# Attention and feed-forward: one interleaved, planned stream in place of two phases

## The chip, the cores and the metric

The kernel runs on one core of a Trainium2 chip. The metric is device time in microseconds (us) of one launch. TensorE (PE, with its weight loads PEld), VectorE (DVE), ScalarE (ACT), GpSimd (POOL) and SyncE (SP, which here only issues DMAs) each run their own instructions in the order in which they stand, and wait for each other by semaphores.

## The reference

q, k, v have 8 batches x 8 heads x 576 rows x 64; the scores are kept in f32. Per head:

```python
scores = 1/sqrt(64) * q @ k.T
thresh = max(scores, axis=-1) - 0.02
scores = where(scores >= thresh, scores, -1e9)
attn   = softmax(scores)                 # over the keys
x[token, head*64:...] = attn @ v         # 4608 tokens x 512
xn  = x / sqrt(mean(x*x) + 1e-6) * rms_g
g   = xn @ w_gate                        # 512 -> 1536
out = (g * sigmoid(g) * (xn @ w_val)) @ w_out     # 1536 -> 512
```

## The kernel before

**Attention.** The loop over `ip` takes 32 pairs of heads. A pair's q and k (f32) are transposed on PE (L96, L104) and copied out by ACT (L114, L115). Then `j` runs over five chunks of query rows (four of 128, one of 64). For a chunk PE makes the scores of both heads against all 576 keys (L134: 512 keys, L136: 64 keys; f32, each head on 64 rows of the array; each f32 matmul shows as two in the trace), ACT the exponential (L141), DVE a copy of the scores with the row maximum (L148), POOL the threshold (L158), DVE mask times exponential and its row sum (L166). One pair later the masked weights are transposed on PE, 128x128 at a time against an f16 identity (L197), copied out by ACT (L208) and multiplied with v into `ot_ps`, which is head dimension x queries (L219, L222). The reciprocal row sums go through a scratch in DRAM (L180) and come back broadcast over the partitions (L185), and L228 writes `xT`, which holds all 4608 tokens.

**Feed-forward.** The attention pools are released; only then do the row norms of all tokens follow (L299 to L306), and then nine blocks of 512 tokens: gate (L329) and value (L331), 12 x 4 matmuls each, sigmoid on ACT (L333), two products on DVE (L335, L338), and the output projection (L343).

**Order.** The tile framework keeps the written order on each engine and adds the waits; buffers in pools set how far one stage may run ahead. Loads of q and k are issued on SP, those of v and of the weights (cast to f16 in flight) on POOL's queue; the weights come first.

Of the kernel before, what the change touches and what calls it, by code (L numbers as in the profile page):

```python
# [13 lines left out]
DEBUG_OUT = None  # L15
# [3 lines left out]
def kernel(  # L19
# [29 lines left out]
    make_identity(nc, id16)
    ones16 = konst.tile([128, 1], FP16, tag="ones16")  # L50
    nc.vector.memset(ones16, 1.0)
    epsk = konst.tile([1, 1], FP32, tag="epsk")
    nc.vector.memset(epsk, 1e-6)
    zrow = konst.tile([128, S], FP16, tag="zrow")
    nc.vector.memset(zrow, 0.0)
    rmsg = konst.tile([128, 4], FP32, tag="rmsg")
    nc.sync.dma_start(out=rmsg, in_=moe_rms_g.rearrange("(c p) -> p c", p=128))

    wpool = ctx.enter_context(tc.tile_pool(name="wpool", bufs=1))
    wg16 = [wpool.tile([128, DFF], FP16, tag=f"wg{dc}", name=f"wg{dc}") for dc in range(4)]  # L60
    wv16 = [wpool.tile([128, DFF], FP16, tag=f"wv{dc}", name=f"wv{dc}") for dc in range(4)]
    wo16 = wpool.tile([128, NFC, DM], FP16, tag="wo16", name="wo16")
    for dc in range(4):
        nc.gpsimd.dma_start(out=wg16[dc], in_=moe_w_gate[128 * dc:128 * (dc + 1)])
        nc.gpsimd.dma_start(out=wv16[dc], in_=moe_w_val[128 * dc:128 * (dc + 1)])
    nc.gpsimd.dma_start(out=wo16, in_=moe_w_out.rearrange("(fc p) d -> p fc d", p=128))

    xt_pool = ctx.enter_context(tc.tile_pool(name="xt", bufs=1))
    xT = [xt_pool.tile([128, B * S], FP32, tag=f"xT{c}", name=f"xT{c}") for c in range(4)]

    p1 = tc.alloc_tile_pool(name="p1", bufs=1)
    p1ps = tc.alloc_tile_pool(name="p1ps", bufs=1, space=bass.MemoryType.PSUM)
    p1dr = tc.alloc_tile_pool(name="p1dr", bufs=1, space=bass.MemoryType.DRAM)

    def big_ps(name):
        return p1ps.tile([128, S], FP32, tag="big", bufs=2, name=name)

    def emit_loads(ip):
        b, c = divmod(ip, 4)
        st = dict(b=b, c=c, ip=ip)  # L80
        st["qsb"] = p1.tile([128, SC, 2, D], FP32, tag="qsb", bufs=2, name="qsb")
        st["ksb"] = p1.tile([128, SC, 2, D], FP32, tag="ksb", bufs=2, name="ksb")
        st["vsb"] = p1.tile([128, SC, 2, D], FP16, tag="vsb", bufs=2, name="vsb")
        for h in range(2):
            for t_dram, t_sb in ((q, st["qsb"]), (k, st["ksb"]), (v, st["vsb"])):
                eng = nc.gpsimd if t_sb is st["vsb"] else nc.sync
                src = t_dram[b, 2 * c + h, 0:512].rearrange("(sc si) d -> si sc d", si=128)
                eng.dma_start(out=t_sb[:, 0:4, h], in_=src)  # L88
                eng.dma_start(out=t_sb[0:64, 4, h], in_=t_dram[b, 2 * c + h, 512:576, :])  # L89
        return st  # L90

    def emit_head_block(st):
        qt_ps = big_ps("qt_ps")
# [15 lines left out]
        st["qt_ps"], st["kt_ps"] = qt_ps, kt_ps

    def emit_qkt_evac(st):
        st["qt"] = p1.tile([128, S], FP32, tag="qt", bufs=2, name="qt")
        st["kt"] = p1.tile([128, S], FP32, tag="kt", bufs=2, name="kt")
        nc.scalar.activation(out=st["qt"], in_=st["qt_ps"], func=AF.Copy, scale=1.0 / 8.0)  # L114
        nc.scalar.copy(out=st["kt"], in_=st["kt_ps"])  # L115
        st["mcol"] = p1.tile([128, 2, 8], FP32, tag="mcol", bufs=2, name="mcol")
        st["zcol"] = p1.tile([128, 2, 16], FP32, tag="zcol", bufs=2, name="zcol")
        st["wsb"] = [p1.tile([128, SC, S], FP16, tag=f"wsb{h}", bufs=2, name="wsb") for h in range(2)]
        st["ssb"] = {}
        st["esb"] = {}  # L120
        st["thr"] = {}
        st["sp"] = {}
        nc.gpsimd.memset(st["zcol"], 1.0)

    def emit_s_matmul(st, j):
        n = CSZ[j]
        lhs, rhs, sp = {}, {}, {}
        for h in range(2):
            sp[h] = big_ps("sp")
            lhs[h] = st["qt"][64 * h:64 * (h + 1), COF[j]:COF[j] + n]  # L130
            rhs[h] = st["kt"][64 * h:64 * (h + 1), :]
            st["sp", h, j] = sp[h]
        for h in range(2):
            nc.tensor.matmul(sp[h][0:n, 0:512], lhs[h], rhs[h][:, 0:512], start=True, stop=True)  # L134
        for h in range(2):
            nc.tensor.matmul(sp[h][0:n, 512:S], lhs[h], rhs[h][:, 512:S], start=True, stop=True)  # L136

    def emit_exp(st, h, j):
        n = CSZ[j]
        e = p1.tile([128, S], FP16, tag="esb", bufs=3, name="esb")  # L140
        nc.scalar.activation(out=e[0:n], in_=st["sp", h, j][0:n], func=AF.Exp)  # L141
        st["esb"][h, j] = e

    def emit_ttr(st, h, j):
        n = CSZ[j]
        sp = st["sp", h, j]
        sc_sb = p1.tile([128, S], FP32, tag="ssb", bufs=3, name="ssb")
# [238 lines left out]
```

## Time and profile before

| | us |
|---|---|
| median of 3 runs (lowest, highest) | 1108.6 (1103.65, 1116.68) |
| span of the profiled execution, first to last instruction | 1101.2 |
| what lies between that span and the median | 7.4 |
| PE busy | 976.1 (89%) |
| DVE busy | 722.0 (66%) |
| ACT busy | 525.0 (48%) |
| POOL busy | 219.0 (20%) |
| mean granted TensorE clock | 0.880 of full speed |

The profiled execution has no time of its own beside its span; the runs are 2.5 to 15.5 us longer than that span. A busy PE is one with a matmul in flight: matmuls are pipelined, and at a granted clock of 0.50 the same work keeps it busy twice as long. A window's granted clock is a mean over it.

### The profile page before, as it was taken

Reading aid. Unit: us, or ns where it says so; the run is one execution under the profiler, and the core shown is the slowest. Engines: PE = TensorE matmul, PEld = TensorE weight load, DVE = VectorE, ACT = ScalarE, POOL = GpSimd, SP = SyncE. Lnnn points to the kernel's source line nnn. Section 1 sums busy time; section 2 is a strip of 40 time slices with the busy share of each in tenths; the row PEclk is TensorE's granted clock in tenths of the full one; section 3 lists DMA queues with packets and bytes.
Section 4 is the critical chain, followed back from the end, with each engine's and each line's share of the span. In section 5 each row is a group of like instructions: output and inputs, shape, how many; then the busy total and the mean of one; then the engine's idle time right before and its main releaser. Section 6 shows DMA issues by size and latency. Waiting matters only on the chain.

```text
span 1101.2 us, 15548 instructions
## 1 busy us (share of the span) xinstructions
PE 976.1 (89%) x5172; PEld 524.3 (48%) x5172; DVE 722.0 (66%) x1640; ACT 525.0 (48%) x896; POOL 219.0 (20%) x497
## 2 busy tenths in 40 slices
PE   0899998898888999899899899988769999999998
PEld 0455555555445555455555555554214444444443
DVE  0566776677667677776676767776595566555544
ACT  0355554556555555555555556555742223333332
POOL 4122223223232222322222322231000000000000
PEclk9998886889888789886787989897559999999999
DMA  9522222332223222323222323210101110111111
GB/s 179 79 40 52 46 38 40 53 60 40 39 42 52 51 47 38 50 44 60 39 39 39 55 41 59 39 20 15 31 20 48 39 39 22 46 49 39 39 39 39
DMA packets 134227, 50.77 MB, mean 46 GB/s; under 512 B 121721, under 2 KB 123257, under 8 KB 134146
## 3 DMA queue, kind: packets, MB, share of 16 engines
q1 hardware_dynamic: 92530, 40.32, 14.2%
q0 software_dynamic: 41616, 9.45, 9.2%
q8 instruction: 41, 0.67, 0.3%
q14 instruction: 40, 0.33, 0.1%
HBM read 49.55 MB, written 9.62 MB: 54 GB/s over the span
## 4 chain that ended last, share of the span: by engine, by line
PE 63%; DVE 11%; issue 9%; ACT 7%; POOL 7%; DMA 2%; SPq 0%; POOLq 0%; ACTq 0%
PE sp L134 17%; PE gps L329 9%; PE vps L331 9%; PE ops L343 8%; PE wt_ps L197 7%; PE ot_ps L219 7%; DVE ssb L148 6%; ACT esb L141 5%; PE sp L136 4%; POOL vsb L88 3%; POOL vsb L89 3%; DVE irow L305 3%; DVE wsb L166 3%; ACT wtsb L208 2%; DMA ksb<-in_k_dram 2%
## 5 line engine op out<-in xcount | busy, mean ns | idle before, releaser
L148 DVE CUSTOM_DVE_ANT_0 ssb<-sp,zrow 128x576 f32<-128x576 f32 (+1 forms) x320 | 229.5, 753 | 161.9 <-ACT esb L141 161.9
L134 PE MATMUL sp<-kt,qt 64*128 64x512 f32 (+1 forms) x640 | 317.7, 797 | 14.3 <-DVE mcol L148 9.0
L166 DVE SCALAR_TENSOR_TENSOR wsb<-ssb,th,esb 128x576 f16<-128x576 f32 (+1 forms) x320 | 259.2, 817 | 48.8 <-POOL th L158 36.6
L141 ACT ACTIVATE esb<-sp 128x576 f16<-128x576 f32 (+1 forms) x320 | 190.8, 646 | 208.3 <-issue 134.6
L197 PE MATMUL wt_ps<-id,wsb 128*128 128x128 f16 (+3 forms) x1600 | 188.8, 244 | 35.0 <-DVE wsb L166 35.0
L208 ACT COPY wtsb<-wt_ps 128x576 f16<-128x576 f16 (+1 forms) x320 | 193.3, 647 | 42.2 <-PE wt_ps L197 41.9
L158 POOL TENSOR_SCALAR th<-mcol 128x1 f32<-128x1 f32 (+1 forms) x320 | 123.0, 384 | 405.9 <-DVE mcol L148 401.3
L197 PEld LDWEIGHTS <-wsb 128*128 128x128 f16 (+3 forms) x1600 | 118.7, 109 | 112.6 <-DVE wsb L166 50.4
L136 PEld LDWEIGHTS sp<-kt,qt 64*128 64x128 f32 (+1 forms) x640 | 122.3, 226 | 78.9 <-issue 71.2
L134 PEld LDWEIGHTS sp<-kt,qt 64*128 64x128 f32 (+1 forms) x640 | 93.1, 213 | 92.2 <-DVE mcol L148 85.2
L335 DVE TENSOR_TENSOR sl<-gps,sg 128x512 f32<-128x512 f32 x108 | 74.6, 691 | 92.0 <-ACT sg L333 92.0
L219 PE MATMUL ot_ps<-wtsb,vsb 128*64 128x512 f16 (+1 forms) x320 | 123.4, 430 | 0.0
L333 ACT ACTIVATE sg<-gps 128x512 f32<-128x512 f32 x108 | 64.5, 597 | 122.7 <-PE gps L329 122.7
L329 PE MATMUL gps<-xn,wg 128*128 128x512 f16 x432 | 113.0, 383 | 9.3 <-DVE xn L319 9.3
L331 PE MATMUL vps<-xn,wv 128*128 128x512 f16 x432 | 112.1, 382 | 0.0
L136 PE MATMUL sp<-kt,qt 64*128 64x64 f32 (+1 forms) x640 | 110.4, 285 | 0.0
L343 PE MATMUL ops<-wo,h 128*128 128x512 f16 x432 | 94.7, 379 | 0.0
L338 DVE TENSOR_TENSOR h<-vps,sl 128x512 f16<-128x512 f32 x108 | 74.6, 691 | 11.0 <-PE gps L329 0.9
L96 PE MATMUL qt_ps<-id,qsb 128*128 128x128 f32 (+1 forms) x160 | 27.7, 287 | 52.8 <-issue 30.3
L329 PEld LDWEIGHTS <-wg 128*128 128x128 f16 x432 | 42.6, 99 | 61.9 <-issue 11.9
L114 ACT ACTIVATE qt<-qt_ps 128x576 f32<-128x576 f32 x32 | 20.8, 651 | 104.6 <-PE qt_ps L96 104.6
L331 PEld LDWEIGHTS <-wv 128*128 128x128 f16 x432 | 42.5, 98 | 52.5 <-issue 2.3
(38 smaller groups left out, 585.3 us busy)
## 6 DMA issues: line engine op xcount, KB each, us to landing
rzbc<-zscr SPq DMA_DIRECT2D x64, 144.0 KB
out_dram<-osb SPq DMA_DIRECT2D x36, 256.0 KB
qsb<-in_q_dram SPq DMA_DIRECT2D x64, 128.0 KB
ksb<-in_k_dram SPq DMA_DIRECT2D x64, 128.0 KB
vsb<-in_v_dram POOLq DMA_DIRECT2D x64, 64.0 KB, 2.8
zscr<-rzt SPq DMA_DIRECT2D x256, 0.6 KB
irb<-irdr SPq DMA_DIRECT2D x9, 256.0 KB
wg<-in_moe_w_gate_dram POOLq DMA_DIRECT2D x4, 384.0 KB, 10.0
```

Source lines behind the costliest of these rows:

```text
L134: nc.tensor.matmul(sp[h][0:n, 0:512], lhs[h], rhs[h][:, 0:512], start=True, stop=True)
L136: nc.tensor.matmul(sp[h][0:n, 512:S], lhs[h], rhs[h][:, 512:S], start=True, stop=True)
L141: nc.scalar.activation(out=e[0:n], in_=st["sp", h, j][0:n], func=AF.Exp)
L148: nc.vector.tensor_tensor_reduce(out=sc_sb[0:n], in0=sp[0:n], in1=zrow[0:n], scale=1.0, scalar=-3.0e38, op0=ALU.add, op1=ALU.max, accum_ou ...
L158: nc.gpsimd.tensor_scalar(out=th[0:n], in0=st["mcol"][0:n, h, j:j + 1], scalar1=-tau, scalar2=None, op0=ALU.add,)
L166: nc.vector.scalar_tensor_tensor(out=st["wsb"][h][0:n, j], in0=st["ssb"][h, j][0:n], scalar=st["thr"][h, j][0:n], in1=st["esb"][h, j][0:n] ...
L197: nc.tensor.transpose(wt_ps[0:nk, COF[qc]:COF[qc] + nq], st["wsb"][h][0:nq, qc, COF[kc]:COF[kc] + nk], id16[0:nq, 0:nq],)
L208: nc.scalar.copy(out=wt[0:nk], in_=st["wt_ps", h, kc][0:nk])
L219: nc.tensor.matmul(ot[64 * h:64 * h + 64, 0:512], lhs, rhs[0:nk, 0:512], start=first, stop=last)
L329: nc.tensor.matmul(g_ps, wg16[dc][:, fsl], xn[dc], start=(dc == 0), stop=(dc == 3))
L331: nc.tensor.matmul(v_ps, wv16[dc][:, fsl], xn[dc], start=(dc == 0), stop=(dc == 3))
L343: nc.tensor.matmul(o_ps, hsb[fc][:, otc[tb]:otc[tb] + 128], wo16[:, fc], start=(fc == 0), stop=(fc == NFC - 1),)
```

## The change

The whole kernel is written anew. What is computed stays, in another order and with other parts:

- The unit is a **step**: 128 query rows x one pair of heads. The 576 rows of a batch give four chunks of 128 ("m"); the left 64 rows of two batches form one more chunk ("v"). That is 36 chunks x 4 pairs = 144 steps, chunk by chunk, so that a chunk's 512 features of x are complete after four steps.
- q is scaled by -1/8, so the row minimum plus tau is the negated threshold. DVE's reduction (L414) reads PSUM and leaves the negated scores in `ssb`. POOL adds tau (L421).
- For head 0 of a step ACT masks with Prelu of slope 1e30 (L430) and takes the exponential (L434). For head 1 ACT takes the exponential (L443), and POOL makes the mask (L457) and multiplies (L462). In the first 16 steps both heads go the first way.
- The masked weights of a step (128 x 1152, f16) are transposed by one DMA on SP (L473) into `wt`, nine blocks of 128. PE multiplies them as the stationary operand with v (L488; L493 for a "v" chunk), whose 64 columns have 64 columns of ones beside them: the row sums come out as columns of `ot`. DVE divides (L514, L515).
- The row norm is taken per chunk: ACT squares and sums (L526), POOL raises to -1/2 (L531), DVE scales (L534), one DMA transposes 128x512 (L537).
- The feed-forward of a group of chunks (512, 256 or 128 tokens) is cut into pieces (gate L576, value L581, output L615), and the pieces stand between the attention's steps; sigmoid is written with tanh (L588), and DVE's products are L591 and L596. Three PSUM banks (`ring`) serve gate, value, output and the transposes of q and k (L266, L292, L309); scores have four banks, `ot` one.
- Weights are loaded in f32 by SP (L671) and multiplied by rms_g into f16 on POOL (L674) between the first steps.
- A planner (`order_ops`) orders all operations before the program is written: each has an engine, a cost out of a table, a priority and its dependencies; of the operations that could start first the one of lowest priority number is taken.

```diff
-    for ip in range(NPAIR + 2):          # attention, pair by pair
-        ... emit_wt_transposes, emit_s_matmul, emit_wt_evac, emit_exp, emit_ttr, emit_th, emit_stt
-    p1ps.release(); p1.release(); p1dr.release()
-    for t in range(NTC): ...             # row norms, then feed-forward
+    def emit_s(s):                       # "m" chunk
+        for lo, n, src in ((512, MAIN, kT[b % 2][p]), (448, TAIL, kTt[b % 2][:, p])):
+            for h in range(2):
+                hs = slice(64 * h, 64 * h + 64)
+                nc.tensor.matmul(s_ps[h][:, lo:lo + n], qT[b % 2][p][hs, 128 * c:128 * (c + 1)],
+                                 src[hs], start=True, stop=True)
+    ...
+    nc.vector.tensor_tensor_reduce(
+        out=ssb[a][:, h], in0=s_ps[h][:, 448:1024], in1=zrow, scale=1.0, scalar=3.0e38,
+        op0=ALU.add, op1=ALU.min, accum_out=mx[m][:, h:h + 1])
+    ...
+    nc.sync.dma_start_transpose(out=wt[s % NWT], in_=wsb[s % NW].rearrange("p h s -> p (h s)"))
+    ...
+    for j in range(5):
+        nc.tensor.matmul(ot[:, cs], w[:, 4 * h + j], v_rhs(b % 2, p, 5 * h + j),
+                         start=(j == 0), stop=(j == 4))
+    ...
+    for s, (ci, p) in enumerate(steps):
+        so = s_of[s] = emit_s(s)
+        emit_softmax(s, so)
+        emit_av(s)
+        if p % 2:
+            emit_half(s)
+        if p == NP - 1:
+            xt_op[ci] = emit_x(ci, s, gi % NXT, 128 * j)
+            if ci in last_of:
+                emit_ffn(last_of[ci] % NXT, [...], s + 5, PACE)
+    ...
+    seq = order_ops(ops, {"R": 3})
+    with tc.manual_schedule():
+        for o in seq:
+            o.fn(o)
+PACE, FIRST, WAYS = 16.0, 16, ("pg",)
```

Where the order moves, PE first, inside the attention. Before (`sp` scores, `wt_ps` transposed weights, `ot_ps` output):

```order
L219 LDWEIGHTS vsb
L219 MATMUL ot_ps<-wtsb,vsb 64x512
L222 LDWEIGHTS vsb
L222 MATMUL ot_ps<-wtsb,vsb 64x64
L134 MATMUL sp<-kt,qt 128x512 x2
L136 MATMUL sp<-kt,qt 128x64 x2
L197 LDWEIGHTS wsb
L197 MATMUL wt_ps<-id_63,wsb 128x128
```

After, on PE about a third of the way through (`s_ps` scores, `wt` weights from the DMA, `ring` transposed k and value piece):

```order
L380 MATMUL s_ps_177<-kTt_99,qT_1_87 128x64
L488 LDWEIGHTS wt_128
L488 MATMUL ot<-va_103,wt_128 128x128
...
L266 MATMUL ring_181<-id_61,kn_77 128x128 x4
L581 LDWEIGHTS wv_69
L581 MATMUL ring_179<-xnT_147,wv_69 128x512
...
L380 MATMUL s_ps_176<-kT_2_96,qT_2_88 128x512
```

No transpose of weights is left on PE, and feed-forward stands between two steps' scores. The `wt` that is read belongs to a step four to five before the scores next to it. The first gate piece stands behind the scores of step 18; behind those of the last step stand 192 feed-forward matmuls of 128 columns, 164 of 256, 72 of 512 and three steps' products with v.

DVE before, inside a pair:

```order
L148 ISA ssb,mcol<-sp,zrow 128x576
L148 ISA mcol 128x1
L148 ISA ssb,mcol<-sp,zrow 128x576
L148 ISA mcol 128x1
L166 SCALAR_TENSOR_TENSOR wsb,zcol<-ssb,th,esb 128x576 x2
L228 TENSOR_TENSOR xT_101<-ot_ps,rzbc 128x576
```

DVE after:

```order
L414 ISA ssb_104,mx_107<-s_ps_176,zrow 128x576
L414 ISA mx_107 128x1
L414 ISA ssb_104,mx_107<-s_ps_177,zrow 128x576
L414 ISA mx_107 128x1
L514 RECIPROCAL rz_131<-ot 128x4
L515 TENSOR_TENSOR xsb_133<-ot,rz_131 128x256
L591 SCALAR_TENSOR_TENSOR sl_154<-th_151,ring_181 128x512
L596 TENSOR_TENSOR hf_160<-ring_179,sl_154 128x512
```

The mask has left DVE, and the feed-forward's products stand between the reductions of two steps.

SP after, in the same stretch (`kn`, `qn`: loads for a later batch):

```order
L262 DMA kn_77<-in_k_dram 128x4x64 x2
L262 DMA qn_75<-in_q_dram 128x4x64 x2
L473 DMA_TRANSPOSE wt_128<-wsb_123 128x9x128
L473 DMA_TRANSPOSE wt_129<-wsb_124 128x9x128
L473 DMA_TRANSPOSE wt_125<-wsb_122 128x9x128
L537 DMA_TRANSPOSE xnT_147<-xn_145 128x4x128
```

Loads, transposes and stores share SP's queue in one order: 144 transposes of nine blocks and 36 of four stand among some 210 plain DMAs.

## Rows read from the trace of the kernel before

**Rows 1.** The page: the span, and PE's busy time, share and instructions.
```profile
span 1101.2 us, 15548 instructions
PE 976.1 (89%) x5172; PEld 524.3 (48%) x5172; DVE 722.0 (66%) x1640; ACT 525.0 (48%) x896; POOL 219.0 (20%) x497
```

**Rows 2.** Stretches: length; PE, PEld, DVE, ACT, POOL busy (count); clock; DMA share; GB/s.
```profile
842.00:873.00 31.00, 31.00 (x145) 14.04 (x144) 19.06 (x28) 9.51 (x16) 0.00 (x0) 1.00 0.12 43
...
200.00:300.00 100.00, 88.53 (x540) 51.32 (x538) 72.85 (x193) 57.04 (x99) 28.54 (x65) 0.92 0.28 49
20.00:28.00 8.00, 2.77 (x10) 1.79 (x10) 0.00 (x0) 0.74 (x2) 1.11 (x2) 1.00 1.20 194
779.00:811.00 32.00, 19.23 (x36) 2.94 (x36) 26.59 (x10) 27.05 (x47) 0.00 (x0) 0.50 0.06 17
```

**Rows 3.** Order of time on PE: start, duration, what; one pair of heads.
```profile
404.56 2.08 PE L134 MATMUL sp<-kt,qt 64*128 64x512 f32 x4
406.43 0.53 PE L136 MATMUL sp<-kt,qt 64*128 64x64 f32 x4
...
408.55 1.37 PE L134 MATMUL sp<-kt,qt 64*128 64x512 f32 x3
409.51 0.33 PE L136 MATMUL sp<-kt,qt 64*128 64x64 f32 x2
...
410.45 0.99 PE L197 MATMUL wt_ps<-id,wsb 128*128 128x128 f16 x10
...
420.25 0.83 PE L96 MATMUL qt_ps<-id,qsb 128*128 128x128 f32 x5 [1.01 <-issue]
421.01 0.86 PE L104 MATMUL kt_ps<-id,ksb 128*128 128x128 f32 x5
```

**Rows 4.** Two short stretches of PE: length, busy (count), granted clock, DMA share, GB/s.
```profile
404.50:406.90 2.40, 2.40 (x11) 0.50 0.57 128
...
408.50:410.50 2.00, 1.95 (x9) 1.00 0.01 2
```

**Rows 5.** Order of time on PE: the first scores.
```profile
28.60 2.08 PE L134 MATMUL sp<-kt,qt 64*128 64x512 f32 x4 [0.73 <-ACT kt L115]
```

**Rows 6.** The chain that ended last: the last block's output projection.
```profile
1087.12 10.38 PE ops L343 x48
```

**Rows 7.** Order of time on DVE and POOL: reductions, mask, threshold.
```profile
403.07 0.76 DVE L148 CUSTOM_DVE_ANT_0 ssb<-sp,zrow 128x576 f32<-128x576 f32 x1 [2.14 <-ACT esb L141]
...
403.75 0.75 DVE L148 CUSTOM_DVE_ANT_0 ssb<-sp,zrow 128x576 f32<-128x576 f32 x1
...
404.00 0.21 POOL L158 TENSOR_SCALAR th<-mcol 128x1 f32<-128x1 f32 x1 [3.12 <-DVE mcol L148]
...
404.43 0.82 DVE L166 SCALAR_TENSOR_TENSOR wsb<-ssb,th,esb 128x576 f16<-128x576 f32 x1
...
404.67 0.64 POOL L158 TENSOR_SCALAR th<-mcol 128x1 f32<-128x1 f32 x1 [0.46 <-DVE mcol L148]
```

**Rows 8.** Groups by shape: line, engine, count; busy us, mean ns; idle before.
```profile
L141 ACT ACTIVATE esb<-sp 128x576 f16<-128x576 f32 x256 | 152.9, 648 | 171.2 <-issue 100.0 <-PE sp L136 67.5 <-DVE wsb L166 1.7
...
L335 DVE TENSOR_TENSOR sl<-gps,sg 128x512 f32<-128x512 f32 x108 | 74.6, 691 | 92.0 <-ACT sg L333 92.0
...
L333 ACT ACTIVATE sg<-gps 128x512 f32<-128x512 f32 x108 | 64.5, 597 | 122.7 <-PE gps L329 122.7
...
masks.py:199 POOL TENSOR_SCALAR_AFFINE_SELECT id<-id 128x128 f32<-128x128 f32 x1 | 0.3, 290 | 0.0
```

**Rows 9.** DMA queues: packets, MB, share; issues: count, KB, us to landing.
```profile
q1 hardware_dynamic: 92530, 40.32, 14.2%
q0 software_dynamic: 41616, 9.45, 9.2%
...
vsb<-in_v_dram POOLq DMA_DIRECT2D x64, 64.0 KB, 2.8
```

**Rows 10.** Order of time on PE: the first transpose.
```profile
22.56 1.38 PE L96 MATMUL qt_ps<-id,qsb 128*128 128x128 f32 x5 [22.56 <-DMA qsb<-in_q_dram]
```

More of the change, by code (lines that the diff above doesn't have):

```diff
@@ L51 @@
[L51 to L69, printed above, removed]
@@ L111, in emit_qkt_evac @@
[L111 to L123, printed above, removed]
@@ new lines, with gated, add @@
+    ops = []
+    gates = []
+    s_of = {}
+    def gated(o, step):
+        gates.append((o, step))
+        return o
+    def add(eng, cost, prio, deps, fn, **kw):
+        o = Op(eng, cost, prio, deps, fn, **kw)
+        ops.append(o)
+        return o
+    chunks = []
+    for i in range(B // 2):
+        chunks += [("m", 2 * i, c) for c in range(4)]
+        chunks.append(("v", i, 0))
+        chunks += [("m", 2 * i + 1, c) for c in range(4)]
+    steps = [(ci, p) for ci in range(len(chunks)) for p in range(NP)]
@@ new lines, with setup, consts, vconst @@
+    first_step = {}
+    for s, (ci, p) in enumerate(steps):
+        kind, b, _ = chunks[ci]
+        if kind == "m":
+            first_step.setdefault(b, s)
+    last_s = {}
+    last_sv = {}
+    last_av = {}
+    n_load = {"q": 0, "k": 0}
+    tr_of = {"q": [], "k": []}
+    k_ready = {}
+    kt_ready = {}
+    q_ready = {}
+    qv_ready = {}
+    v_ready = {}
+    tail_load = {}
+    def setup():
+        o_id = add("POOL", 2000.0, -100, [], lambda o: make_identity(nc, id32))
+        def consts(o):
+            nc.vector.memset(zrow, 0.0)
+            nc.vector.memset(mhalf, -0.5)
+        def vconst(o):
+            for i in range(2):
+                nc.vector.memset(va[i][:, :, 10:13], 1.0)
+                for j in (4, 11):
+                    nc.vector.memset(va[i][64:128, :, j], 0.0)
+                for j in (5, 12):
+                    nc.vector.memset(va[i][0:64, :, j], 0.0)
+        o_c = add("DVE", 300.0, -100, [], consts)
+        o_v = add("DVE", 2000.0, -90, [], vconst)
+        o_g = add("SP", 70.0, -50, [], lambda o: nc.sync.dma_start(
+            out=rmsg, in_=moe_rms_g.rearrange("(c p) -> p c", p=128)), dma=100.0)
+        return o_id, o_c, o_v, o_g
@@ L354 @@
+    for o, step in gates:
+        if step > 0:
+            o.deps.append(s_of[int(step)])
+    for h in range(2):
+        ttr_of[len(steps) - 1, h].opens = (3 + 2 * h, 4 + 2 * h)
+    seq = order_ops(ops, {"R": 3})
+    global LAST_SEQ
+    LAST_SEQ = seq
+    with tc.manual_schedule():
+        for o in seq:
+            o.fn(o)
+PACE = 16.0
+FIRST = 16
+WAYS = ("pg",)
+PRELU = AF.Prelu
+PRELU_KW = dict(alpha=1.0e30)
 _INS = ['q', 'k', 'v', 'tau', 'moe_w_gate', 'moe_w_val', 'moe_w_out', 'moe_rms_g']
```

743 lines of the change are left out of this document (491 added, 252 removed).

## The prediction, made before the changed kernel was run

> **What bounds the kernel now.** I read the page's first part first: PE is busy 976 us of a span of 1101.2, every other engine far less [rows 1]. Then the busy time by stretches [rows 2]. In the feed-forward (842 to 873) PE is busy without a break at full granted clock; in the attention (200 to 300) it is busy 88.5 us of 100 at clock 0.92; between the two, 779 to 811, it works 19 us of 32 at half clock while the row norms of all tokens are made. So PE is the bound in both big phases, but in the attention part of its time is half clock, and part is work that is no product of the reference: the transposes of the weights. That half clock doubles a duration is seen in two neighbouring pieces of one pair: the scores that begin at 404.56 take 1.87 us until their tail of 64 keys starts, at clock 0.50; those at 408.55 take 0.96, at 1.00 [rows 3, 4]. The scores at 28.60 last as the half-clock ones do [rows 5].
>
> The sum is made against the profiled execution. It has its span, 1101.2; the median of the runs, 1108.6, lies 7.4 above, and I add those 7.4 to every span below.
>
> **PE's work after the change, at full clock.** Counts are those of the new order.
> - Scores of a step: half of the half-clock piece, which is 406.43 + 0.53 - 404.56 = 2.40 us for both heads [rows 3], so 1.20. 128 steps of an "m" chunk are 154 us; a "v" chunk's step does the same twice (16 x 2.40 = 38). Sum 192.
> - Products with v: 1600 matmuls of 128 columns, each with a load of its own. No row has this form. From below: a 512-column matmul of the output projection takes 10.38 / 48 = 0.216 us [rows 6], a quarter is 0.054. From above: ten weight transposes of the same size, loads included, take 0.99 [rows 3], 0.099 each. The first price supposes that the loads hide, the second holds what they cost there; I take the middle, 0.077: 123 us.
> - Transposes of q and k: 304, at (421.01 - 420.25) / 5 = 0.152 [rows 3]: 46 us.
> - Feed-forward: (576 + 432) matmuls of 512 columns at 0.216, 480 of 256 at 0.108, 192 of 128 at 0.077: 218 + 52 + 15 = 285 us.
>
> Sum 645 us, against 976 busy now. What goes is the weight transposes, the half clock, and scores of half-empty chunks (five per batch and pair, now four and a half).
>
> **The other engines stay below that.** DVE: 288 reductions at 403.75 - 403.07 = 0.68 [rows 7] are 196 us; the feed-forward's products at 0.691 for 512 columns [rows 8], 144 of them, are 100, and the 168 of 256 or fewer at some 0.43 (estimate, between a half and the whole) 72; what remains (division, norm: 72 and 36 small operations) is below 80. Sum some 450. ACT: 427 passes over 576 columns at 0.648 [rows 8] are 277, the tanh at 0.597 or less some 80, copies and squares 144 x 0.65 = 94: some 450. POOL now gets the mask and the multiply of one head per step, of which before shows nothing of this size. From below, an operation on one column takes 0.21 [rows 7]; from above, a select over 128 columns takes 0.29 [rows 8], times 4.5 for 576 is 1.3, and twice that for the one with two inputs, 2.6. With a threshold of 0.21 to 0.64 a step costs POOL between 0.6 and 4.5 us, PE's mean step in the middle is 4.7 (below). So POOL is not the bound even at its upper end, but close to it there. The threshold is 0.21 beside a reduction that reads PSUM, and 0.64 beside the mask on DVE [rows 7], which the change removes; I count the lower one.
>
> **The DMA transposes** have no row at all. A step moves 128 x 1152 x 2 = 294,912 bytes. From below: at the 194 GB/s that loads reach [rows 2], 1.5 us. From the packets: the hardware queue spends 0.142 x 16 x 1101.2 / 92530 = 0.027 us an engine and packet, the software queue 0.039 [rows 9]. In pieces of 256 bytes (a row of 128) a transpose is 72 packets an engine, 1.9 to 2.8 us; in pieces of 64 bytes, 288, 7.8 us. I take 2, since the order shows one instruction for nine blocks with rows of 128. With the 36 smaller ones there are 160 equivalents: 320 us, and the other transfers fill at most what all do now, 0.234 x 1101 = 258 [rows 9]. That is 578 of some 730: no bound. As latency they cost nothing: a step's products with v stand four to five steps behind its scores, some 20 us; the reductions (1.4), threshold (0.2), ACT (3 x 0.65), POOL and a transfer with its landing (2.8 for a load [rows 9]) need about 11. If that cover is gone, PE stands at the first load of `wt`, with all feed-forward behind it.
>
> The Trainium skill speaks against this part. In "VectorE: DVE Perf Modes", section "The three transpose paths", a 128x128 transpose takes 1309 ns by the DMA crossbar and 390 on TensorE, and its table of rules prefers TensorE where PSUM will do as the target; nine blocks in a row would be 11.8 us, and the DMA work alone 160 x 11.8 = 1,890 us, not 320. No row here shows such a transfer.
>
> **The sum, in three stretches.**
> - Until the feed-forward starts (19 steps). PE now waits until 22.56 for its first q, behind the weights [rows 10]; afterwards q and k are in front, and I put the first scores at 13 (a landing of 2.8 for loads, three transposes with their copies, and slack). A step then is a loop: scores, two reductions, next scores. At half clock, which [rows 5] shows for a start, that is 2.40 + 1.36 + 0.3 for hand-offs = 4.1; at full clock 2.9. I take 3.9: 13 + 19 x 3.9 = 87. PE does 48 us of its 645 in it.
> - The middle. What stands behind the last scores is 192 x 0.077 + 164 x 0.108 + 72 x 0.216 + 30 x 0.077 = 50, so the middle holds 645 - 48 - 50 = 547, or 4.4 us a step for 125 steps. While DVE reduces (1.4) PE has 3.2 us of other work a step, so the loop through DVE closes in time. Hand-offs that don't: now PE idles 11.5% of the attention [rows 2]; most engines then waited on one pair, here steps overlap, and I take 5%, with clock 0.98: 547 / 0.95 / 0.98 = 588.
> - The end: 50 and a last copy and store, 55.
>
> 87 + 588 + 55 = 730, plus 7.4: **737 us**, 0.66 of before.
>
> **Rivals.**
> 1. *Everything cheaper.* Products with v at 0.054, no idle in the middle, clock 1.00, early steps at 2.9. Total work 604; 68 + 514 + 50 + 7 = 639. For it: PE in the feed-forward shows no break at all [rows 2]. Against: the mix has many short waits.
> 2. *PE in the middle as in today's attention.* Busy 0.885, clock 0.92, early steps at 4.1: 547 / 0.814 = 672; 91 + 672 + 57 + 7 = 827. For it: hand-offs among four engines, three shared PSUM banks, strict order. Against: the breaks now lie between pairs (PE idle 1.01 before the transposes of q at 420.25 [rows 3]), and there are no such boundaries afterwards.
> 3. *The feed-forward doesn't overlap.* The order puts it between steps, but if each piece only comes through where attention stands still, the change doesn't do what it says: 13 + 144 x 3.9 + 285 + 7 = 867.
> 4. *The DMA transposes bound it* (the side of slower). One mechanism: the crossbar path moves small pieces, the sixteen DMA engines fill, `wt` comes late, PE waits at each load of it. Time is 160 x (time of one) + 258 + some 20; it is slower than before from 5.2 us for one, and at 7.8 gives 1,526. For it: no row excludes small packets; those of the two queues now average 436 and 227 bytes [rows 9]. Against: 256-byte rows are as natural, and give 2 us. At the skill's 11.8 us it would be some 2,170; of the 9% below I give that price 3.
>
> **Chances and range.** Forecast (670 to 790) 60%, rival 1 14%, rival 2 12%, rival 3 5%, rival 4 9%. The range of 8 in 10 goes from rival 1 to rival 3: 640 to 865, which leaves out rival 4 and the rims. A change of 1% (11 us) is about what a measurement of this kernel can tell from none. Faster by over 1%: 90%; within 1%: 1%; slower by over 1%: 9%.
>
> **What would show it.** PE busy near 645 us and the bound (over 85% of a span near 730); matmuls of `ot` at 0.05 to 0.1 apart; scores of a step in 1.2 us at clock 1.00; the first gate matmul near 87 us; some 55 us from the last scores to the end; DMA busy share near 0.8 at most, transposes landing within 5 us. It is wrong if PE waits most for `wt` (rival 4), if the time of PE before L380 ends on DVE for more than a tenth of the middle (rival 2), or if POOL turns out busiest, its two operations having cost over 4 us a step.

## The result, and the profile of the changed kernel

Measured on one chip, four runs each: **701.8 us** (700.12 to 703.25) for the changed kernel, 1106.4 (1103.65 to 1116.68) for the kernel before. The ratio is 0.633, 95% interval 0.630 to 0.637. The forecast was 737, range 640 to 865. The profiled execution of the changed kernel has a run time of 701.5 us and a span of 699.8, so what lies around the span is 1.7 us here, where 7.4 were added. (The 7.4 set one execution's span against the median of others; in all later runs, of both kernels, 1.7 to 2.2 us lie around an execution's own span.) The ratios here and below are taken over executions in the faster of two states in which the chip ran these kernels; in the session of experiments 5 to 8 three of the seven executions of the kernel before were in the slower one, and the 693.0 of experiment 10 was.

First the page of the changed kernel: the span, then busy time, share and instructions of each engine; the granted clock and the DMA share in 40 slices; the two DMA queues; the chain of waits by engine.

```profile
span 699.8 us, 13808 instructions
PE 641.8 (92%) x4864; PEld 388.6 (56%) x4864; DVE 428.8 (61%) x1080; ACT 455.2 (65%) x789; POOL 529.3 (76%) x570
...
PEclk9897889998899999999999999999999999999999
DMA  9899997487686546975897455977596454444410
...
q1 hardware_dynamic: 275344, 81.83, 59.1%
q0 software_dynamic: 14912, 6.30, 8.7%
...
PE 45%; POOL 29%; issue 8%; DMA 6%; ACT 6%; DVE 4%; SPq 1%; POOLq 0%; DVEq 0%; ACTq 0%
```

PE is busy 642 us where it was 976 [rows 1] and still has the largest share. New is POOL: 529 us where it had 219, and 29% of the chain. The chain names PE and POOL together, which says that two engines are close to their limit; it does not say what either is worth. Experiments 2 and 3 settle that.

Next the stretches, in the columns of [rows 2]: before the first scores (their first matmul begins at 11.1), until the first gate matmul (90.7), the middle until the last scores' matmul is done (646), the end.

```profile
0.00:11.10 11.10, 2.44 (x10) 1.70 (x11) 2.93 (x12) 2.48 (x3) 6.03 (x14) 1.00 0.94 144
11.10:90.70 79.60, 62.06 (x374) 40.31 (x373) 31.27 (x87) 53.72 (x90) 49.67 (x58) 0.82 1.05 206
90.70:646.00 555.30, 529.03 (x4027) 310.98 (x4025) 363.04 (x881) 377.26 (x639) 466.52 (x492) 0.98 0.67 123
646.00:699.80 53.80, 48.26 (x458) 35.61 (x457) 31.55 (x102) 21.79 (x58) 7.11 (x8) 1.00 0.21 52
```

In the middle PE works 529 of 555 us at clock 0.98, where the attention of before stood at 88.5% and 0.92 [rows 2]; POOL works 467, 84%.

Then the order of time on PE (start, duration, what), in three places: the first gate; one step's scores; ten products with v among feed-forward pieces near the end.

```profile
90.71 1.03 PE L576 MATMUL ring<-xnT,wg 128*128 128x256 f16 x4
...
299.99 1.13 PE L380 MATMUL s_ps<-kT,qT 64*128 64x512 f32 x4
300.95 0.33 PE L380 MATMUL s_ps<-kTt,qT 64*128 64x64 f32 x4
301.22 1.04 PE L581 MATMUL ring<-xnT,wv 128*128 128x512 f16 x4
...
650.67 0.73 PE L488 MATMUL ot<-va,wt 128*128 128x128 f16 x10
651.24 0.60 PE L576 MATMUL ring<-xnT,wg 128*128 128x256 f16 x4
```

Matmuls are pipelined, so a price is the distance from one start to the next, not a duration. A step's scores take 301.22 - 299.99 = 1.23 us. Ten products with v take 651.24 - 650.67 = 0.57, so 0.057 each, their loads included.

POOL's order of time in the same place, where the steps' operations follow each other almost without a gap:

```profile
299.11 1.28 POOL L462 TENSOR_TENSOR wsb<-wsb,esb 128x576 f16<-128x576 f16 x1
300.46 0.22 POOL L421 TENSOR_SCALAR nth<-mx 128x2 f32<-128x2 f32 x1
300.78 1.73 POOL L457 TENSOR_SCALAR wsb<-ssb,nth 128x576 f16<-128x576 f32 x1
302.59 1.27 POOL L462 TENSOR_TENSOR wsb<-wsb,esb 128x576 f16<-128x576 f16 x1
303.85 1.71 POOL L457 TENSOR_SCALAR wsb<-ssb,nth 128x576 f16<-128x576 f32 x1
```

The mask takes 1.73 us, the multiply 1.28, the threshold 0.22: 3.2 us a step, against 4.4 that a step of the middle lasts (555.3 / 125). Last the page's row of the DMA transposes: count, and us from issue to landing.

```profile
wt<-wsb SPq DMA_TRANSPOSE x144, 3.3
```

### The profile page after: what moved, and what is told of

Its sections match the earlier page's. It is cut to its first block, busy times and chain, and to the rows that moved or that the text cites. A ratio compares the mean times of both kernels' runs of the same rounds, so it can differ in the third digit from the quotient of the medians.

```text
span 699.8 us, 13808 instructions
## 1 busy us (share of the span) xinstructions
PE 641.8 (92%) x4864; PEld 388.6 (56%) x4864; DVE 428.8 (61%) x1080; ACT 455.2 (65%) x789; POOL 529.3 (76%) x570
## 3 DMA queue, kind: packets, MB, share of 16 engines
q1 hardware_dynamic: 275344, 81.83, 59.1%
## 4 chain that ended last, share of the span: by engine, by line
PE 45%; POOL 29%; issue 8%; DMA 6%; ACT 6%; DVE 4%; SPq 1%; POOLq 0%; DVEq 0%; ACTq 0%
POOL wsb L457 13%; PE s_ps L380 12%; POOL wsb L462 8%; PE ring L615 8%; PE ring L576 6%; PE ring L581 6%; DMA wt<-wsb 5%; PE ot L488 5%; POOL nth L421 2%; ACT ssb L430 2%; DVE ssb L414 2%; PE ring L266 2%; PE ot L493 2%; POOL wv L674 2%; ACT wsb L434 1%
## 5 line engine op out<-in xcount | busy, mean ns | idle before, releaser
L414 DVE CUSTOM_DVE_ANT_0 ssb<-s_ps,zrow 128x576 f32<-128x576 f32 x288 | 208.4, 753 | 135.8 <-PE s_ps L380 91.9
L457 POOL TENSOR_SCALAR wsb<-ssb,nth 128x576 f16<-128x576 f32 x128 | 221.6, 1731 | 9.1
L380 PE MATMUL s_ps<-kT,qT 64*128 64x512 f32 x512 | 172.3, 676 | 15.0 <-DVE mx L414 9.9
L462 POOL TENSOR_TENSOR wsb<-wsb,esb 128x576 f16<-128x576 f16 x128 | 163.4, 1277 | 11.3 <-ACT esb L443 1.9
L443 ACT ACTIVATE esb<-ssb,nth 128x576 f16<-128x576 f32 x128 | 98.8, 772 | 95.0 <-POOL nth L421 94.6
L430 ACT ACTIVATE ssb<-ssb,nth 128x576 f32<-128x576 f32 x160 | 121.0, 762 | 12.4 <-POOL nth L421 12.4
L581 PE MATMUL ring<-xnT,wv 128*128 128x512 f16 (+2 forms) x528 | 108.4, 328 | 2.6 <-DVE sl L591 1.8
L488 PE MATMUL ot<-va,wt 128*128 128x128 f16 x1280 | 97.4, 226 | 14.6 <-DMA wt<-wsb 12.0
L434 ACT ACTIVATE wsb<-ssb 128x576 f16<-128x576 f32 x160 | 107.6, 680 | 3.9
L576 PE MATMUL ring<-xnT,wg 128*128 128x512 f16 (+2 forms) x520 | 107.3, 329 | 0.9 <-ACT qT L273 0.7
L588 ACT ACTIVATE th<-ring 128x512 f32<-128x512 f32 (+2 forms) x130 | 63.0, 488 | 57.2 <-PE ring L576 57.0
L488 PEld LDWEIGHTS <-wt 128*128 128x128 f16 x1280 | 80.3, 101 | 34.8 <-DMA wt<-wsb 21.8
L591 DVE SCALAR_TENSOR_TENSOR sl<-th,ring 128x512 f32<-128x512 f32 (+2 forms) x130 | 71.9, 553 | 45.1 <-ACT th L588 43.1
L421 POOL TENSOR_SCALAR nth<-mx 128x2 f32<-128x2 f32 x144 | 34.6, 240 | 81.6 <-DVE mx L414 61.6
L380 PEld LDWEIGHTS s_ps<-kTt,qT 64*128 64x128 f32 x512 | 62.3, 196 | 60.3 <-issue 58.5
L615 PE MATMUL ring<-wo,hf 128*128 128x512 f16 x396 | 90.3, 379 | 0.0
L596 DVE TENSOR_TENSOR hf<-ring,sl 128x512 f16<-128x512 f32 (+2 forms) x132 | 73.7, 558 | 12.1 <-PE ring L581 2.4
L380 PEld LDWEIGHTS s_ps<-kT,qT 64*128 64x128 f32 x512 | 48.8, 194 | 57.3 <-DVE mx L414 26.5
L581 PEld LDWEIGHTS <-wv 128*128 128x128 f16 x624 | 54.6, 98 | 33.4 <-issue 4.6
L576 PEld LDWEIGHTS <-wg 128*128 128x128 f16 x624 | 55.2, 98 | 31.4 <-issue 1.7
L615 PEld LDWEIGHTS <-hf 128*128 128x128 f16 x432 | 40.7, 98 | 44.9 <-issue 0.2
L380 PE MATMUL s_ps<-kTt,qT 64*128 64x64 f32 x512 | 54.0, 252 | 0.0
```

Of the source, the lines that this page charges most:

```text
L380: nc.tensor.matmul(s_ps[h][:, lo:lo + n], qT[b % 2][p][hs, 128 * c:128 * (c + 1)], src[hs], start=True, stop=True)
L414: nc.vector.tensor_tensor_reduce(out=ssb[a][:, h], in0=s_ps[h][:, 448:1024], in1=zrow, scale=1.0, scalar=3.0e38, op0=ALU.add, op1=ALU.min, ...
L430: nc.scalar.activation(out=ssb[a][:, h], in_=ssb[a][:, h], func=PRELU, scale=-1.0, bias=nth[m][:, h:h + 1], **PRELU_KW)
L434: nc.scalar.activation(out=wsb[s % NW][:, h], in_=ssb[a][:, h], func=AF.Exp)
L443: nc.scalar.activation(out=esb[es], in_=ssb[a][:, h], func=AF.Exp, scale=-1.0, bias=nth[m][:, h:h + 1])
L457: nc.gpsimd.tensor_scalar(out=wsb[s % NW][:, h], in0=ssb[a][:, h], scalar1=nth[m][:, h:h + 1], scalar2=None, op0=ALU.is_le)
```

## The experiments

They are numbered as they ran; 8, 10 and 11 stand last. The ratio of each is to the kernel before, run on the same chip. The medians of the kernel before in those sessions, 1101.8 to 1111.3, lie up to 5 us on either side of the 1106.4 above, so a small difference from the change is judged by the ratios. Unless said otherwise, the fence holds rows of that kernel's page, as shown above.

**1. Products with v made twice.** What is PE's work worth?

```diff
-            for h in range(2):
+            for h in (0, 0, 1, 1):
```

> Edit: every product with v is made twice (the second time over the first), same order otherwise. It adds 1600 matmuls of 128 columns with their loads on TensorE, 1600 x 0.057 us (ten take 0.57 us in the trace of the change) = 91 us, and nothing elsewhere. Theory A (TensorE's own work sets the middle; it is busy 95% there): nearly all of it shows, 702 + 75 to 95, so 775 to 797 us. Rival B (GpSimd's mask and multiply set the pace: they are 21% of the chain that ended last and GpSimd is 84% busy in the middle): TensorE has slack behind them, 702 to 730 us.

Measured: 750.1 us (745.8 to 753.0), ratio 0.682 [0.677, 0.688].

```profile
span 746.6 us, 17008 instructions
PE 701.0 (94%) x6464; PEld 459.5 (62%) x6464; DVE 428.2 (57%) x1080; ACT 456.7 (61%) x789; POOL 529.2 (71%) x570
...
PE 68%; POOL 17%; issue 5%; DMA 4%; ACT 2%; DVE 2%; SPq 0%; POOLq 0%; DVEq 0%; ACTq 0%
```

1600 products at 0.057 are 91 us of work; the time rose by 48, which is neither of the two expected bands. PE's busy time rose by only 59. The mean clock went from 0.966 to 0.988, which is worth some 14 us of the missing 32 (an estimate: 642 x 0.966 / 0.988); the other 18 no row here accounts for. Of the 59, 12 went into PE's gaps, whose share of the span fell from 8% to 6%. PE's added work counts for about half.

**2. POOL's mask made twice in every second step.** What is POOL's work worth?

```diff
-                        nc.gpsimd.tensor_scalar(...)        # mask, head 1
+                        for _ in range(1 + s % 2):
+                            nc.gpsimd.tensor_scalar(...)
```

> Edit: GpSimd makes the mask of every second step twice (same result), same order otherwise: 64 x 1.73 = 111 us more on GpSimd, nothing elsewhere. Theory A (TensorE sets the middle): GpSimd goes from 467 of 555 us in the middle to some 577, so it just becomes the longer one; 702 + 20 to 40, so 720 to 745 us. Rival B (GpSimd sets the pace): all 111 us show, 800 to 815 us.

Measured: 803.4 us (801.4 to 804.2), ratio 0.731 [0.725, 0.736]. 64 masks at 1.73 are 111 us on POOL, and 102 of them came through. The page:

```profile
PE 677.4 (84%) x4864; PEld 403.3 (50%) x4864; DVE 431.4 (54%) x1080; ACT 454.8 (57%) x789; POOL 639.4 (80%) x634
...
POOL 51%; PE 24%; issue 10%; DMA 6%; DVE 4%; ACT 4%; SPq 1%; POOLq 0%; DVEq 0%; ACTq 0%
```

And the group of PE's products with v in the stretch 90 to 690 (L489 here, L488 in the change; behind the bars: busy us, mean ns; idle before, and what ended it):

```profile
L489 PE MATMUL ot<-va,wt 128*128 128x128 f16 x1000 | 78.2, 229 | 51.3 <-DMA wt<-wsb 48.8 <-DVE mx L414 1.6 <-DVE xsb L516 0.7
```

The idle is put down to the DMA, but the transposes land as soon as before (3.3 us): they start late, behind POOL. In the change the same group has 13 us of idle, 12 for `wt` (below). SP's longest waits there before a transpose are for POOL: for the threshold they grew from 110 to 148 us, for the multiply from 31 to 66. The expectation that POOL has room fell. More work on POOL costs nearly its whole length, at a lower clock of PE as well (0.927).

**3. No mask on POOL: both heads by Prelu on ACT.**

```diff
-PACE, FIRST, WAYS = 16.0, 16, ("pg",)
+PACE, FIRST, WAYS = 16.0, 16, ("pp",)
```

> Edit: head 1 of a step goes the way of head 0 in all steps (both masks by ScalarE), GpSimd keeps only the small operations; the planner orders anew. GpSimd loses 128 x (1.73 + 1.28) = 385 us of 529, ScalarE gains 128 x (0.76 + 0.68 - 0.77) = 86 us to some 541. Theory A: TensorE's work is the same, 690 to 715 us. Rival B: the pace is freed, 640 to 670 us.

Measured: 685.6 us (684.0 to 689.3), ratio 0.625 [0.620, 0.629], between the two expected bands.

```profile
span 682.3 us, 13340 instructions
PE 636.5 (93%) x4864; PEld 391.2 (57%) x4864; DVE 416.8 (61%) x1080; ACT 532.4 (78%) x917; POOL 143.7 (21%) x314
...
PE 66%; ACT 13%; DMA 8%; DVE 5%; issue 4%; POOL 3%; SPq 1%; DVEq 0%; ACTq 0%; POOLq 0%
```

386 us leave POOL, ACT takes 77 more, and 16 us are gained (some 10 by the ratios): PE, now 66% of the chain, stands right behind. Experiments 2 and 3 together give the size that the chain could not: POOL has no slack for more, and giving its mask to ACT is worth 1 to 2%.

**4. The mask on DVE.** `WAYS = ("pd",)`.

> Edit: the mask and multiply of head 1 in one operation on VectorE instead of two on GpSimd; the planner orders anew. VectorE gains 128 x 0.82 = 105 us to some 534, GpSimd loses 385. Theory A: 690 to 715 us as long as VectorE's longer queue doesn't delay the reductions on which the next scores wait. Rival B: 640 to 670 us. A third outcome, VectorE as the new limit through its place in the loop scores - reduction - scores: 720 to 760 us.

Measured: 698.8 us (697.8 to 700.1), ratio 0.636 [0.632, 0.640]; no difference from the change. POOL fell to 180 us, DVE rose to 505: a POOL without the mask gains nothing that can be told if DVE has to make it.

**5. Every DMA transpose made twice**, the second into a buffer that nobody reads. Does the DMA bound it?

```diff
             nc.sync.dma_start_transpose(out=wt[s % NWT], ...)
+            nc.sync.dma_start_transpose(out=wt2[s % NWT], ...)
```

> Edit: every DMA transpose of a step is issued twice, the second into a buffer that nobody reads; same order otherwise. From the packets of the change (its hardware queue: 275344 packets, some 194000 of them transposes, 0.023 us each an engine) one transpose is some 1.7 us of all 16 DMA engines, so 144 x 1.7 = 245 us more on engines that are 68% busy of 700 now: 476 + 245 = 721 us of DMA work, over 1.0 in the first 90 us. My pricing of the prediction (a DMA bound from the sum of transfers): 730 to 790 us. Rival: a transpose is latency, hidden by the four to five steps' lead, 702 to 712 us. Second rival: it costs SyncE 1.3 us to issue one, and the queue, not the engines, becomes late; then the waits for wt on TensorE grow from 34 us while the DMA share stays below 0.9.

Measured: 766.1 us (762.2 to 769.1), ratio 0.696 [0.691, 0.701], within the band priced from the sum of transfers.

```profile
span 762.8 us, 13999 instructions
PE 655.7 (86%) x4864; PEld 395.9 (52%) x4864; DVE 427.9 (56%) x1080; ACT 456.5 (60%) x789; POOL 530.0 (69%) x570
...
DMA  9999999999999998899999999999999998979611
...
q1 hardware_dynamic: 445840, 124.31, 88.3%
q0 software_dynamic: 14912, 6.30, 7.4%
```

q1's time grew from 0.591 x 699.8 = 414 us to 0.883 x 762.8 = 674, so 144 transposes cost 260, **1.8 us each** with all sixteen engines. Now the DMA row is full: 0.957 x 762.8 = 730 us. In the change the same sum is 0.678 x 699.8 = 474. PE's waits for `wt` grew from 16 to 55 us. That fits DMA engines that set the end, but it does not settle it: the share is no hard limit (it was 1.05 in the second stretch of the change), the transposes land in 3.5 us, little later than before (3.3), and SP's queue, on which each takes some 1.3 us to issue, got 144 more as well. The run does not part the engines from the queue.

**6. The feed-forward in lumps.** `PACE = 1.0` in place of 16: a group's pieces come close behind each other.

> Edit: PACE 16 to 1, so the planner no longer spreads a group's feed-forward over 16 steps but lets all of it in as early as it can; work is the same. If the even spread is what makes the gain (TensorE's feed-forward under the attention's waits): lumps of some 31 us of feed-forward, limited by three PSUM banks, and between them steps at the attention's own pace (GpSimd 3.5 us a step), 780 to 880 us. Rival: the planner starts whatever can start first, so attention and feed-forward still mix and it stays at 702 to 740 us.

Measured: 777.4 us (776.1 to 778.4), ratio 0.706 [0.701, 0.711], between the two expected bands and close to the upper one; PE busy 687 us at a mean clock of 0.929. The same instructions in a less even order cost 76 us, of which 45 are PE's longer busy time.

**7. The kernel before, with its weights transposed by DMA.** Is that alone the gain? PE's transposes (L197) and ACT's copies (L208) go; behind each mask stands

```diff
+        nc.sync.dma_start_transpose(
+            out=st["wtT"][h][:, :, COF[j]:COF[j] + n], in_=st["wsb"][h][0:n, j])
```

> Edit on the kernel before, one part of the change alone: the masked weights are transposed by DMA (per head and chunk of query rows, 128 or 64 x 640), in place of TensorE's transposes and ScalarE's copies; everything else stays. It takes 1600 transposes (189 us busy, some 150 at full clock) from TensorE and 320 copies (193 us) from ScalarE. Theory: TensorE bounds the attention of before, 22.7 us a pair, so a pair falls by 3 to 5 us: 1102 - 95 to 160 = 940 to 1005 us. Rival 1: the chain scores - exponential - reduction - mask of one chunk sets the pair (VectorE is busy 16.6 of 22.8), 1060 to 1110 us. Rival 2: the transposes come late and TensorE waits for them at the first product of a pair, slower than 1110 us.

Measured: 1286.5 us (1285.6 to 1287.9), ratio 1.169 [1.162, 1.176]. Slower, which only rival 2 allowed, and its mechanism is not what the trace shows: PE waits 3 us in all for the transposes. PE lost 1600 matmuls but only 38 us of busy time, at a mean clock of 0.717 (before 0.880). What grew are two waits: PE's for DVE's reductions before L141 (L134 before), from 9 to 226 us, and DVE's for POOL's threshold before the mask, from 37 to 150, some 5 us at each of 31 pairs. One such break, from that trace in order of time:

```profile
612.96 0.81 POOL L94 DMA_DIRECT2D vsb<-in_v_dram  x1 [7.28 <-PE ot_ps L218]
...
615.71 0.49 POOL L165 TENSOR_SCALAR th<-mcol 128x1 f32<-128x1 f32 x2
...
615.95 0.84 DVE L173 SCALAR_TENSOR_TENSOR wbuf<-ssb,th,esb 128x576 f16<-128x576 f32 x1 [4.46 <-POOL th L165]
...
618.27 2.75 PE L141 MATMUL sp<-kt,qt 64*128 64x512 f32 x4 [4.38 <-DVE mcol L155]
```

POOL stands at a load of v, which waits for the products that read the old v; the thresholds come behind the four loads, the mask behind the thresholds, the next reductions behind the mask, and PE idles 4.4 us. No run takes these loads off POOL's queue, so what this order costs is not measured.

**9. The same, with the DMAs of the reciprocal row sums on POOL's queue,** in case they stand on SP's queue behind a transpose that waits for its mask.

```diff
-                nc.sync.dma_start(out=scr[h, :, a], ...)
+                nc.gpsimd.dma_start(out=scr[h, :, a], ...)
-            nc.sync.dma_start(out=rzbc[64 * h:64 * (h + 1)], ...)
+            nc.gpsimd.dma_start(out=rzbc[64 * h:64 * (h + 1)], ...)
```

> Edit on the kernel before with DMA transposes (1286.5 us): the reciprocal row sums go out to scratch and come back through GpSimd's queue instead of SyncE's, where the second broadcast stood behind a transpose that waits for the mask of the next pair. If that place in SyncE's queue is what made it slower (VectorE's division waits for the broadcast, the reductions stand behind the division, the next scores behind those; TensorE idles 4.4 us there and falls to half clock): a pair falls from 28.5 us to under 22.7, 950 to 1100 us in all. Rival: the half clock of a TensorE that is left with little work is the cause, it stays at 1200 to 1290 us.

Measured: 1293.9 us (1290.9 to 1295.4), ratio 1.163 [1.158, 1.169], clock 0.715. The place on SP's queue alone is not the cause. The test is not clean, since it put 164 us of issuing on POOL (218 to 382 us busy), where the thresholds stand.

**12. Experiment 7 with PE's transposes back, unread.** Products still take the DMA's copy; ACT copies nothing.

> The kernel before with its weights transposed by DMA (1286.5 us, mean clock 0.717) gets its 1,600 weight transposes on PE back, but nobody reads what they make: the products still take the DMA's copy, and ACT copies nothing. It tells the half clock from the loop. Theory C (with little to do PE stands at half clock, and that makes the pair 28.5 us long): PE gets work between the scores, the mean granted clock rises to 0.80 or more, and the time falls in spite of the added work, to 1110-1230 us. Rival D (a loop through DVE, POOL and the DMA transposes sets the pace; the clock only follows): 1260-1310 us, whatever the clock does. Rival E (PE's work is the bound): 1,600 matmuls at 0.1 to 0.2 us come on top, 1400 us or more.

Measured: 1306.4 us (1301.6 to 1314.6), ratio 1.183 [1.172, 1.194]. Two stretches of the attention in one trace (columns of [rows 2]): nearly all of it, then from a break between two pairs on.

```profile
60.00:960.00 900.00, 763.39 (x3667) 409.80 (x3665) 495.02 (x1312) 223.86 (x366) 200.03 (x453) 0.65 0.47 85
...
422.00:424.00 2.00, 2.00 (x14) 1.20 (x13) 1.76 (x5) 0.16 (x1) 1.21 (x2) 1.00 0.49 109
424.00:428.00 4.00, 0.90 (x6) 0.38 (x3) 2.23 (x7) 1.30 (x2) 1.87 (x5) 0.95 0.66 47
428.00:450.00 22.00, 20.75 (x89) 11.15 (x91) 11.86 (x34) 4.85 (x8) 3.52 (x9) 0.50 0.39 82
```

1600 added matmuls changed the time by 20 us and lifted the clock only from 0.717 to 0.731, so "PE has too little to do" fell. PE goes into the break at 2.4 GHz and comes out at 1.2. It then works 94% of 22 us at the lower level. The band of rival D, a loop as the pace, held. One chunk at that level, in the same trace:

```profile
412.40 2.08 PE L141 MATMUL sp<-kt,qt 64*128 64x512 f32 x4
...
414.27 0.53 PE L143 MATMUL sp<-kt,qt 64*128 64x64 f32 x4
...
414.88 1.19 ACT L148 ACTIVATE esb<-sp 128x576 f16<-128x576 f32 x2 [4.87 <-issue]
...
415.57 0.76 DVE L155 CUSTOM_DVE_ANT_0 ssb<-sp,zrow 128x576 f32<-128x576 f32 x1 [2.96 <-ACT esb L148]
...
416.25 0.75 DVE L155 CUSTOM_DVE_ANT_0 ssb<-sp,zrow 128x576 f32<-128x576 f32 x1
...
417.93 0.63 PE L224 MATMUL ot_ps<-wtT,vsb 64*64 64x512 f16 x1
418.49 2.08 PE L141 MATMUL sp<-kt,qt 64*128 64x512 f32 x4
```

Scores, exponential, two reductions: 416.25 + 0.75 - 412.40 = 4.6 us before a score bank is free again, and 6.1 until the next scores; a pair has five rounds. But here the next scores do not wait for that loop: PE's own products and transposes reach up to them, and in the whole run PE waits 19 us for reductions before its scores, against 226 in experiment 7, and 86 for masks before its unread transposes. So the two runs, with PE busy 763 and 611 of those 900 us, come near the same time by different waits; rival D's loop is seen in experiment 7, and here only its band held. Why the lower level lasts so long with DMA transposes in this structure, and not in the kernel before, no run here shows. Transfers alone are not it: in experiment 5 the DMA row is full and the clock 0.935.

**8. The planner's table with measured durations** (mask 800 to 1730 ns, weight cast 900 to 1570, and so on).

> Edit: the planner's table gets the durations of the trace of the change (mask on GpSimd 1730 for 800 ns, multiply 1280 for 1400, reduction 680 for 850, weight cast 1570 for 900, v load issue 700 for 1300, scores 1220 for 1080 and so on); the work is the same, the order new. The two runs before show that 111 us more on GpSimd cost 102 us although it idles 16% of the middle, and 91 us more on TensorE cost 48. If GpSimd's late results come from a plan that thinks its mask half as long (ScalarE waits 95 us for the threshold behind it), the new order gives 670 to 695 us. Rival: GpSimd's work itself is the limit, 698 to 710 us.

Measured: 697.6 us (695.0 to 699.5), ratio 0.634 [0.630, 0.638]: no difference from the change that can be told, and between the two expected bands, so neither reading of POOL's lateness is borne out by it.

**10. The same table, head 1 by turns on POOL and by Prelu.** `WAYS = ("pg", "pp")`.

> Edit: measured costs in the planner and head 1's mask on GpSimd only in every second step, on ScalarE in the others. GpSimd loses 192 us of 529, ScalarE gains 43 to some 498. If both TensorE and GpSimd are near their limits (the runs with twice the products and twice the masks), and GpSimd alone gets room: 675 to 688 us, as with no mask on GpSimd (685.6). If ScalarE's 532 us had become the limit there, this is lower than that run, 660 to 675.

Measured: 688.4 us (682.2 to 693.0), ratio 0.618 [0.613, 0.622]. The interval is apart from the change's, not from experiment 3's.

**11. The same table, no mask on POOL, and the weights cast on DVE.** `WAYS = ("pp",)` and

```diff
-                    nc.gpsimd.tensor_scalar(out=w_sb[d][:, 512...
+                    nc.vector.tensor_scalar(out=w_sb[d][:, 512...
```

> Edit: measured costs, no mask on GpSimd, and the 24 weight casts on VectorE instead of GpSimd, on whose queue they stand for 37 of the first 90 us with the thresholds behind them (24% of the chain of waits in that stretch). Theory: the first stretch is set by those casts and by ScalarE behind the thresholds; the feed-forward starts 8 to 15 us earlier, 670 to 680 us. Rival: the first stretch is bound by the transfers (DMA share 1.05 in it), 683 to 690 us.

Measured: **677.3 us** (676.0 to 684.1), ratio 0.611 [0.607, 0.615], faster than both kernels. From the change and from experiment 3 its interval is apart, from experiment 10 not. Its first gate matmul comes at 85.9 us, in experiment 3 at 92.8: 7 of the 8 us between the two spans lie there, a little less than the 8 to 15 expected. The casts and the new table differ together from experiment 3.

```profile
span 674.2 us, 13353 instructions
PE 633.3 (94%) x4864; PEld 386.1 (57%) x4864; DVE 425.1 (63%) x1104; ACT 532.5 (79%) x917; POOL 107.3 (16%) x290
...
PE 76%; DMA 8%; DVE 6%; ACT 5%; issue 3%; SPq 1%; POOL 0%; DVEq 0%; ACTq 0%
```

## Why the prediction was right, and where a size was off

**PE stays the bound, with much less work: right.** 645 us forecast, 642 measured, 92% of the span; the mean clock is 0.966. That the two numbers agree so well is partly luck: the products with v were priced too high, and the forecast is at full clock while the busy time has some half clock in it. Nor is PE the bound alone: added work costs about half of its length on PE (experiment 1) and nearly all of it on POOL (experiment 2).

**The stretches.** Until the first gate 87 forecast, 90.7 measured: the first scores came at 11.1 (13 taken) and 19 steps took 79.6, so 4.2 each (3.9 taken), at clock 0.82. The number is near, the mechanism only in part: the loop that was priced (scores, two reductions, next scores) left PE 7 us of waiting for DVE before L380, and the chain of waits in that stretch gives 24% to POOL's weight casts (L674), which the prediction did not price and which experiment 11 moved. The end: 55 forecast, 53.8 measured. The middle: 588 forecast, 555 measured. Its two factors were right: busy 529 / 555 = 0.953 (0.95 taken), clock 0.98 (0.98 taken).

**The term that was mis-sized: products with v.** Taken 0.077 each, between 0.054 and 0.099; measured 0.057, near the bound from below. The loads hide behind the matmuls. The middle holds 1440 of them (L488 and L493, rows below); by 0.02 that is 29 us, nearly all of the 33 by which the middle was off. The scores (1.23 for 1.20) were as taken. The 35 us between 737 and 702 are thus 33 of the middle, 6 of what lies around the span and 1 of the end, less 4 that the start took longer (rounded). Taking the middle of two bounds was the weak step: PE in the feed-forward showed no break with a load for every matmul [rows 2], and that row spoke for the lower one, though each load there had a matmul of 512 columns beside it and not of 128.

**POOL: one bound too low, one sentence too strong.** The mask was bounded by 0.21 and 1.3 and took 1.73; the multiply, at 1.28, lies inside, and so does a whole step: 3.2 us between 0.6 and 4.5. But the sentence that POOL is not the bound even at its upper end was wrong as a reading: it compared a mean step with a mean step. POOL works 84% of the middle, and what it issues late makes `wt` late. Added work costs nearly its length (experiment 2), removed work is worth 10 to 16 us if ACT takes it (experiment 3). So POOL is a second limit beside PE's, and that the forecast held with the mask priced too low is partly luck. A smaller slip: ACT's 427 passes over 576 columns are 448 in the trace (160 each of L430 and L434, 128 of L443); its sum, 450 for 455, came out all the same.

**DMA transposes: 2 us taken, 1.8 measured,** from pieces of 256 bytes as taken: of q1's 275,344 packets the second set in experiment 5 added 170,496, 1,184 for a transpose of 294,912 bytes, 249 bytes each. The DMA share is 0.68 in all, below the 0.8. The Trainium skill ("VectorE: DVE Perf Modes", section "The three transpose paths") has 1309 ns for a 128x128 transpose through the DMA crossbar, nine blocks in a row 11.8 us by my estimate. The trace does not agree: nine blocks in one instruction cost 1.8 us of the sixteen engines and land 3.3 us after their issue.

**Rival 4 has the right mechanism and did not come about.** Experiment 5 comes close to it: with the transposes doubled, the DMA row is full, PE waits longer for `wt` and the time rises by 64 us, though SP's queue may share in that. One transpose would have had to cost some twice as much. Its sign, that PE waits most for `wt`, was badly put. In the middle PE's longest idle is indeed for `wt`, yet it is small, as the first two groups show in the columns of experiment 2 (the third, the scores, is for the next paragraph):

```profile
L488 PE MATMUL ot<-va,wt 128*128 128x128 f16 x1120 | 83.2, 222 | 13.0 <-DMA wt<-wsb 11.8 <-DVE xsb L515 0.7
...
L493 PE MATMUL ot<-va,wt 128*64 128x128 f16 x320 | 13.9, 227 | 4.2 <-DMA wt<-wsb 4.2
...
L380 PE MATMUL s_ps<-kT,qT 64*128 64x512 f32 x448 | 141.6, 659 | 3.0 <-DVE mx L414 2.7
```

These are rows of 90.7 to 646. 16 us of 555 do not make the DMA the bound, and experiment 2 shows that late work on POOL gives the same row; the sign needed a size and a cause.

**Rivals 2 and 3 fell.** PE idles 4.7% of the middle, not 11.5%; before L380 it waits 2.7 us for DVE, where a tenth of the middle was the mark. The feed-forward overlaps: it is spread over the 555 us, and experiment 6 shows that the even spread is worth 76 us, far more than any term of the sum that was argued over.

**What the gain is made of.** The forecast counted removed transposes, full clock and fuller chunks together. Experiments 7 and 9 show that the first alone gives nothing in the old structure: there the DMA transposes in place of PE's made it 16 to 17% slower, with a mean clock of 0.62 in the attention, that is, PE mostly at 1.2 GHz. What pays is an order in which PE has something else to do. Of that, experiment 6 shows 76 us, for the even spread of the feed-forward; how the rest of the 405 us divides between the removed work, the clock and the overlap no run parts.

## What to carry to other kernels

Price a stream of matmuls by the distance between starts in a stretch without breaks; here a load for each matmul was hidden, at 0.057 us for 128 columns, and the middle of two bounds is no estimate if a row tells which it is near. Taking work off the bound engine paid here only where other independent work was in line for it: DMA transposes of the weights are part of a gain of 37% in the interleaved stream and a loss of 17% in the old loop. Look too at what else stands in the queue of an engine that is hardly busy: POOL's loads of v, ahead of the thresholds, kept PE waiting in experiment 7. When the chain of waits names two engines, add work to each and take it away from one before tuning either.

## What the runs showed of the hardware

- A DMA transpose of 128 x 1152 f16 in SBUF: 1.8 us of all sixteen engines (experiment 5), landing 3.3 us after issue (the change).
- On POOL a compare of 576 f32 columns with a scalar of its own row, written as f16, took 1.73 us; a multiply of two f16 tiles of that size only 1.28.
- PE can stand at the lower clock level while it is busy 94% of 22 us (experiment 12), and 76 us of order alone went with a fall of the mean clock from 0.966 to 0.929 (experiment 6).
